# Gated mix of dilated window attention and full attention: row-maxima products of the projection stage on 32 rows of the array instead of 64

## The chip, the cores and the metric

One Trainium2 chip, one core of it. The metric is the device time of one execution in microseconds (us). Engines are named as in the profile: PE is TensorE's matmuls and PEld its weight loads, DVE is VectorE, ACT is ScalarE, POOL is GpSimd, SP is SyncE, which issues the DMAs.

## The reference: what is computed

`x` is 2048 tokens by 448 features. Two attention blocks with 16 heads of 28 read the same `x`, each with its own `wqkv` and `wo`. Block A lets a token see 8 earlier tokens, two apart; block B is full attention. A gate per token mixes them.

```python
def _A_ref(x, wqkv, wo):            # W, dil = 8, 2
    ...
    idx = pos[:, None] - off[None, :]        # off = arange(8) * 2
    logits = jnp.einsum("bhsd,bhswd->bhsw", q, kg) * scale
    ...
def _B_ref(x, wqkv, wo):
    ...
    scores = jnp.einsum("bhqd,bhkd->bhqk", q, k) * (Dh ** -0.5)
    p = _softmax(scores, axis=-1)
    o = jnp.einsum("bhqk,bhkd->bhqd", p, v)
    ...
x = A_x
g = _sigmoid((x * gate_w).sum(-1, keepdims=True))
return g * _A_ref(x, A_wqkv, A_wo) + (1 - g) * _B_ref(x, B_wqkv, B_wo)
```

## The kernel before, in words

The kernel writes the order of every engine by hand. It has two long stages on PE, and a short end in which the two output projections run beside the last attention steps.

**Projection stage.** `x` and the weights are split into a high and a low part (`xh`, `xl`, `wh`, `wl`), and a product of the two is the sum of three products, so a tile of 128 output rows takes 11 matmuls (the list `ORDER`; four of 128 input features for high by high, four for low weights, three for low inputs). There are 92 tiles: 28 for queries and keys of block B (`"qk"`, 512 columns, line 293), 16 for its values (`"v"`, 448 columns, line 298) and 48 for block A (`"a"`, 448 columns, line 298). The first 10 tiles (`FULL`) run as matmuls over all 128 rows of the array. From tile 10 on `project_halves` cuts every product into two of 64 input features: one uses the array's rows 0 to 63 and writes `PJ[n % 2][:, 0, :]`, the other uses rows 64 to 127 and writes `PJ[n % 2][:, 1, :]`. Two lists (`todo[0]` and `todo[1]`, one for each half of the array) are popped in turn, so consecutive matmuls use different halves. For two tiles there are 21 products in each list. ACT then copies both sums out of PSUM, and POOL adds them.

**Row maxima.** Block B's softmax subtracts, per query, the maximum of its scores over the keys. These maxima come from products of their own (`s1`), one matmul for 128 queries by 512 keys of one head, 1024 in all, on the high parts alone. Number `n` is divided into a block `u` of 512 queries and four heads, 128 queries of it, 512 keys of it, and a head `h = n % 4`. Each result is 512 wide in PSUM, and DVE reduces it to one number per query in `MX`. 320 of the 1024 run in the projection stage, four for each of the 80 tiles 12 to 91; the other 704 run in the attention stage.

In the attention stage a maxima product reads the 28 rows of its head: `slice(32 * h, 32 * h + DH)`. In the projection stage it reads 64 rows: heads 0 and 1 lie in rows 0 to 63 of `KH`, heads 2 and 3 in rows 64 to 127, and the queries lie in two tiles, `QP[..][0]` with heads 0 and 2 and `QP[..][1]` with heads 1 and 3, whose other rows are zero. So a product over 64 rows sums one head alone. `s1_half(k, half)` issues one such matmul for head `k + 2 * half` into `PM[k][:, half, :]`. It stands in list `half`: `k = 0` after two products of the tile, `k = 1` after eight entries. When both halves have issued their `k`, DVE reduces `PM[k]`, two heads by 512, in one instruction (line 162).

**Attention stage.** 256 steps, each with 12 score matmuls over 28 or 30 rows (line 1022; four heads, three products each), up to three maxima products over 28 rows (line 144), then eight matmuls of probabilities by values over 128 rows and 32 columns (line 976, two for each of four heads). ACT exponentiates the scores (line 1025), DVE reduces maxima (line 148), and POOL does block A. The end projects with `wo` (line 815, 128 rows).

Of the kernel before, what the change touches and what calls it, by code (L numbers as in the profile page):

```python
# [11 lines left out]
ALU = mybir.AluOpType  # L12
X = mybir.AxisListType.X
ET = mybir.EngineType

S, D, H, DH = 2048, 448, 16, 28
# [5 lines left out]
NMX = 192  # L22
# [3 lines left out]
def gated_mix_kernel(ctx: ExitStack, tc: tile.TileContext, xT, xn, gw, wA, wB, woAB, out):  # L26
    nc = tc.nc
# [26 lines left out]
    PJ, PM = PS[0:2], PS[2:4]  # L54
# [20 lines left out]
    MX = cp.tile([128, NMX], F32, name="MX")  # L75
# [13 lines left out]
    half = {}  # L89
# [37 lines left out]
    s1c = [0]  # L127
    s1e = 64 * NU
    finished = []

    def load_qhi(u):
        g, b = divmod(u, NB)
        qhis[u] = QP[u % 2]
        for h in range(4):
            r = 112 * g + DH * h
            dma_r(qhis[u][h % 2][32 * h:32 * h + DH, :], qk_hi[r:r + DH, 512 * b:512 * b + 512])

    def s1_mm(n, bank, half=False):
        u, i = divmod(n, 64)
        qs, kc, h = i // 16, i // 4 % 4, i % 4  # L140
        if i == 0 and u + 1 < NU:
            load_qhi(u + 1)
        r = slice(64 * (h // 2), 64 * (h // 2) + 64) if half else slice(32 * h, 32 * h + DH)
        nc.tensor.matmul(bank, qhis[u][h % 2][r, 128 * qs:128 * qs + 128],  # L144
                         KH[u // NB % 3][r, 512 * kc:512 * kc + 512], start=True, stop=True)

    def s1_max(n, k, bank):
        r = nc.vector.tensor_reduce(MX[:, n % NMX:n % NMX + k], bank, axis=X, op=ALU.max)  # L148
        if n // 64 != (n + k) // 64:
            finished.append(n // 64)  # L150
        s1c[0] = n + k
        return r.ins


    def s1_half(k, half):
        n = s1c[0]
        s1_mm(n + k + 2 * half, PM[k][:, half, :], True)
        halves[k] += 1
        if halves[k] == 2:
            halves[k] = 0  # L160
            m = MX[:, n % NMX:n % NMX + 4].rearrange("p (a b) -> p a b", b=2)[:, :, k]
            nc.vector.tensor_reduce(m, PM[k], axis=X, op=ALU.max)  # L162
            if k == 1:
                s1c[0] = n + 4
                if s1c[0] % 64 == 0:
                    finished.append(n // 64)

    halves = [0, 0]

# [12 lines left out]
    def max_turn(t):  # L184
        r = sp.tile([128, 32], F32, name="nms")
        nc.vector.transpose(r, t)
        return r
# [18 lines left out]
    with tc.tile_pool(name="xp", bufs=1) as xp, tc.tile_pool(name="wp", bufs=2) as wp:  # L206
# [103 lines left out]
        def project_halves(n, s1):  # L310
            if n % 2 == 0:
                for m in (n, n + 1):
                    low = (tiles[m][2] if tiles[m][1] == "qk" else tiles[m][-1] // 4) < 2
                    for half in range(2):
                        l = [p for p in ORDER if p != (0, 1, 3) or half == (0 if low else 1)]
                        l = [(m, product, (m, p, half, i == 0, i == len(l) - 1)) for i, p in enumerate(l)]
                        if s1[m - n]:
                            late = m == S1_START
                            l[8 + late:8 + late] = [(m, s1_half, (1, half))]
                            l[2 + 4 * late:2 + 4 * late] = [(m, s1_half, (0, half))]  # L320
                        todo[half] += l
            while any(l and l[0][0] == n for l in todo):
                for l in todo:
                    if l:
                        _, f, x = l.pop(0)
                        f(*x)
# [83 lines left out]
        r, t = xst[:, 0, 0:3, :], xst[:, 0, 3, :]  # L410
# [7 lines left out]
        for kt in range(3):  # L418
            nc.vector.tensor_tensor(out=xl[0][:, kt, :], in0=r[:, kt, :], in1=xh[0][:, kt, :].bitcast(F32),
                                    op=ALU.subtract)  # L420
        nc.vector.tensor_tensor(out=tail[64:128], in0=t[64:128], in1=tail[64:128].bitcast(F32), op=ALU.subtract)
        nc.vector.tensor_tensor(out=wl0[:, 3, 0:256], in0=wt0[:, 0:256], in1=wh0[:, 3, 0:256].bitcast(F32),
                                op=ALU.subtract)
# [27 lines left out]
        for n, t in enumerate(tiles):  # L451
# [4 lines left out]
            for w in splits:  # L456
                i, k = (n - splits[w][0]) * splits[w][1], splits[w][1]
# [6 lines left out]
            if n < FULL:  # L464
                project(n)
            else:
                project_halves(n, [S1_START <= m < S1_START + 80 for m in (n, n + 1)])
# [41 lines left out]
            if n == 70:  # L509
                r = max_turn(omw)  # L510
# [175 lines left out]
    for c in range(8):  # L686
# [20 lines left out]
        n = 0  # L707
# [10 lines left out]
    late = {"pool": 0.0, "dve": 0.0}  # L718
# [186 lines left out]
    for u in range(NU - 1):  # L905
        f = NJ * (u + 1)
        l = {NU - 3: (1, 2, 5, 6, 9, 12, 13, 15), NU - 2: (1, 2, 5, 6, 8, 10, 10, 12)}.get(
            u, (1, 3, 6, 8, 12, 18, 19, 22) if u < NU - 5 else (1, 3, 6, 8, 12, 15, 16, 19))
# [88 lines left out]
    def scores(u, kt, cur):  # L997
# [10 lines left out]
        for tok in WITH if k else ALONE:  # L1008
            if tok[0] == "s":
                i = int(tok[1])  # L1010
                if i < k:
                    s1_mm(n + i, bank[tok])
                if i == 0:
                    s1_max(n, 1, T1)
                elif i == 2 and k > 1:
                    r = s1_max(n + 1, k - 1, other[:, 0:k - 1, :])
                    apart(r, other)
                continue
            a, t = tok[0], int(tok[1])
            h = (int(a) + n) % 4  # L1020
            r = slice(32 * h, 32 * h + (DH + 2 if t == 0 else DH))
            nc.tensor.matmul(bank[a], (KH[g % 3], KH[g % 3], KL[g % 2])[t][r, ks], (qh, ql, qh)[t][r, :], start=(t == 0), stop=(t == 2))  # L1022
            if t == 2 and a in "20":
                p = probs[len(exps) % 8]
                e = nc.scalar.activation(p, RP[0] if a == "2" else mine, AF.Exp, scale=SCALE).ins  # L1025
                if len(exps) >= 8:
                    tc.declare_no_dep(e, exps[-8], reason="the matmuls that read it came between")
                exps.append(e)
                if a == "0":
                    apart(e, mine)  # L1030
                cur[(h + 3) % 4], cur[h] = p[:, 0, :], p[:, 1, :]
                yield len(cur)
# [17 lines left out]
    for u in range(NU):  # L1050
        g, b = divmod(u, NB)
# [62 lines left out]
    for j in range(12, 16):  # L1114
# [4 lines left out]
        bank = acc[j - 12]  # L1119
# [40 lines left out]
```

## Time and profile before

| | us |
|---|---|
| median of 3 runs (lowest, highest) | 914.49 (913.26, 914.99) |
| the profiled execution | 912.73 |
| its span, first to last instruction | 911.0 |
| PE busy | 903.8 (99%) |
| DVE busy | 731.7 (80%) |
| ACT busy | 652.2 (72%) |
| POOL busy | 620.6 (68%) |

The profiled execution is 1.76 us below the median, and 1.73 us of it lie outside its span. A PE record runs from the start of a matmul to the modelled end of its results, so records overlap and a busy PE is not a PE at its peak; the distance from start to start is what a matmul costs. A PEld record is the load of weights that stands ahead of every matmul. Shapes such as 64\*128 are rows by columns of the array that the instruction uses. In a timeline, consecutive instructions of the same kind are merged into one row with their count, and a bracket names the idle time before the row and what ended it; "issue" means that nothing that the profile shows was waited for.

### The profile page before, as it was taken

The page shows a single profiled execution, that of the slowest core. Times are in us where ns is not written, and L with a number is a line of the kernel's source. Part 1 is how long each engine was busy: PE and PEld are TensorE (multiplying, and loading weights), DVE is VectorE, ACT ScalarE, POOL GpSimd, SP SyncE. Part 2 cuts the span into 40 slices and gives each one's busy share as a digit, 9 for nine tenths or more (in the row PEclk, how much of TensorE's full clock was granted, in tenths as well). Part 3 has the DMA queues.
Part 4 walks back from the last instruction along what each step waited for, and adds up shares of the span by engine and source line. Part 5 has one row for each costly group of instructions (what it writes and reads, how often), then busy time and mean ns, then how long its engine had stood idle before and what let it go on. Part 6 is the DMA issues. An engine that isn't in the chain of part 4 may idle for free.

```text
span 911.0 us, 20699 instructions
## 1 busy us (share of the span) xinstructions
PE 903.8 (99%) x8396; PEld 536.3 (59%) x8396; DVE 731.7 (80%) x977; ACT 652.2 (72%) x802; POOL 620.6 (68%) x485
## 2 busy tenths in 40 slices
PE   9999999999999999999999999999999999999998
PEld 7889999999944444444444444444444444466667
DVE  6488999999989998999999999999998888401012
ACT  6456434343388898888888888888989989855551
POOL 2489846564469799998999999999996762300100
PEclk9999999999999999999999999999999999999999
DMA  9977403554373331426135242341311223554422
GB/s 266 294 260 197 133 12 89 155 132 117 82 244 91 95 103 45 113 82 143 34 109 146 82 103 73 96 111 44 92 44 36 55 69 100 143 162 120 134 83 91
DMA packets 101119, 104.29 MB, mean 114 GB/s; under 512 B 61652, under 2 KB 71252, under 8 KB 100240
## 3 DMA queue, kind: packets, MB, share of 16 engines
q1 hardware_dynamic: 100880, 102.72, 39.8%
q8 instruction: 65, 1.06, 0.5%
q10 hardware_dynamic: 144, 0.26, 0.1%
q14 instruction: 30, 0.25, 0.1%
HBM read 61.99 MB, written 40.48 MB: 112 GB/s over the span
## 4 chain that ended last, share of the span: by engine, by line
PE 95%; DMA 1%; ACT 1%; SPq 1%; DVE 0%; issue 0%; POOL 0%; ACTq 0%; DVEq 0%; POOLq 0%
PE T L1022 29%; PE av L976 27%; PE r L298 15%; PE T L815 8%; PE r L293 7%; PE r L144 4%; PE T L144 4%; ACT P L1025 1%; PE T L793 1%; DMA V<-in_xT 1%; DMA onlo<-on_lo 1%; SPq L101 0%; DMA rs<-finv 0%; SPq L854 0%; ACT wo L758 0%
## 5 line engine op out<-in xcount | busy, mean ns | idle before, releaser
L1025 ACT ACTIVATE P<-T 128x1024 f32<-128x1024 f32 x512 | 497.7, 1026 | 81.9 <-PE T L1022 80.3
L148 DVE TENSOR_REDUCE MX<-T 128x1 f32<-128x512 f32 x470 | 441.5, 954 | 31.2 <-PE T L144 18.7
L976 PE MATMUL av<-P,V 128*32 128x512 f32 x2048 | 272.7, 605 | 0.3
L1022 PEld LDWEIGHTS T<-QH,KH 30*128 30x128 f32 x1024 | 90.8, 181 | 221.2 <-ACT P L1025 198.2
L144 PE MATMUL T<-KH,QP 28*128 28x512 f32 x704 | 219.6, 454 | 0.3 <-DVE MX L162 0.3
L1022 PE MATMUL T<-QH,KH 30*128 30x512 f32 x1024 | 212.0, 489 | 1.2 <-ACT P L1025 1.1
L162 DVE TENSOR_REDUCE MX<-r 128x2 f32<-128x1024 f32 x160 | 192.6, 1221 | 24.6 <-PE r L144 22.9
L1022 PE MATMUL T<-QH,KL 28*128 28x512 f32 x1024 | 186.4, 396 | 0.0
L1022 PE MATMUL T<-QL,KH 28*128 28x512 f32 x1024 | 184.1, 392 | 0.0
L611 POOL TENSOR_TENSOR prod<-qt,kt 128x896 f32<-128x896 f32 x64 | 135.1, 2114 | 1.8 <-DMA kt<-a_scr 1.8
L362 ACT ACTIVATE raw<-r 128x896 f32<-128x896 f32 (+1 forms) x64 | 58.9, 921 | 97.8 <-PE r L298 96.5
L666 POOL TENSOR_TENSOR oat<-oat,prod 128x896 f32<-128x896 f32 x56 | 118.2, 2110 | 2.3
L144 PEld LDWEIGHTS T<-KH,QP 28*128 28x128 f32 x704 | 86.0, 181 | 27.3 <-ACT P L1025 22.0
L661 POOL TENSOR_TENSOR prod<-vt,L 128x896 f32<-128x896 f32 x56 | 95.4, 1704 | 0.4
L363 POOL TENSOR_TENSOR ast<-raw 128x448 f32<-128x448 f32 x48 | 55.4, 1154 | 58.2 <-ACT raw L362 47.1
L1022 PEld LDWEIGHTS T<-QL,KH 28*128 28x128 f32 x1024 | 93.4, 184 | 0.0
L1022 PEld LDWEIGHTS T<-QH,KL 28*128 28x128 f32 x1024 | 91.9, 183 | 0.9
L976 PEld LDWEIGHTS av<-P,V 128*32 128x32 f32 x2048 | 40.3, 108 | 77.6 <-issue 72.5
L298 PE MATMUL r<-wh,xh 64*128 64x448 f32 (+1 forms) x512 | 83.5, 362 | 0.0
L144 PE MATMUL r<-KH,QP 64*128 64x512 f32 x320 | 83.1, 390 | 0.0
L803 DVE TENSOR_TENSOR oalo<-T,oah 128x384 fp32r<-128x384 f32 x16 | 8.9, 557 | 90.8 <-ACT onhi L802 87.7
L298 PE MATMUL r<-wh,xl 64*128 64x448 f32 (+1 forms) x384 | 69.4, 363 | 0.0
(110 smaller groups left out, 1104.0 us busy)
## 6 DMA issues: line engine op xcount, KB each, us to landing
a_scr<-ast SPq DMA_DIRECT2D x24, 448.0 KB
qk_hi<-qkh SPq DMA_DIRECT2D x24, 256.0 KB
qk_lo<-qkh SPq DMA_DIRECT2D x24, 256.0 KB
rbc<-rs SPq DMA_DIRECT2D x60, 64.0 KB
QP<-qk_hi SPq DMA_DIRECT2D x64, 56.0 KB
KL<-qk_lo SPq DMA_DIRECT2D x16, 224.0 KB
QH<-qk_hi SPq DMA_DIRECT2D x64, 56.0 KB
QL<-qk_lo SPq DMA_DIRECT2D x64, 56.0 KB
```

Source lines behind the costliest of these rows:

```text
L144: nc.tensor.matmul(bank, qhis[u][h % 2][r, 128 * qs:128 * qs + 128], KH[u // NB % 3][r, 512 * kc:512 * kc + 512], start=True, stop=True)
L148: r = nc.vector.tensor_reduce(MX[:, n % NMX:n % NMX + k], bank, axis=X, op=ALU.max)
L162: nc.vector.tensor_reduce(m, PM[k], axis=X, op=ALU.max)
L293: nc.tensor.matmul(bank, ws[c][rows, k, t[4]:t[4] + 128], x, start=first, stop=last)
L298: nc.tensor.matmul(bank[:, 0:cols], x, ws[c][rows, k, 0:cols], start=first, stop=last)
L611: nc.gpsimd.tensor_tensor(out=p, in0=qt[c], in1=kvt["k", c % 2][:, HALO - DIL * w:HALO - DIL * w + NJ, :], op=ALU.mult)
L661: nc.gpsimd.tensor_tensor(out=dst.rearrange("p j (h d) -> p j h d", d=DH), in0=kvt["v", c % 2][:, HALO - DIL * w:HALO - DIL * w + NJ, :].r ...
L666: nc.gpsimd.tensor_tensor(out=oat[c], in0=oat[c], in1=oat[c, w], op=ALU.add)
L815: writes(bank, nc.tensor.matmul(bank[:, :D], src, wo[c][:, k, :], start=(first and k == ks[0] and i == 0), stop=(last and k == ks[-1] and ...
L976: nc.tensor.matmul(av[32 * h:32 * h + 32, :], V[:, kt, 4 * g + h, :], tiles_[h], start=(kt == 0), stop=(kt == NJ - 1), skip_group_check=True)
L1022: nc.tensor.matmul(bank[a], (KH[g % 3], KH[g % 3], KL[g % 2])[t][r, ks], (qh, ql, qh)[t][r, :], start=(t == 0), stop=(t == 2))
L1025: e = nc.scalar.activation(p, RP[0] if a == "2" else mine, AF.Exp, scale=SCALE).ins
```

## The change

It touches the 320 maxima products of the projection stage. `s1_mm` loses its argument `half` and always reads the 28 rows of its head, so that these matmuls use 32 rows of the array, a quarter, in place of 64. `s1_half` is replaced by `s1_two(half)`: it issues two of them one behind the other, heads `2 * half` and `2 * half + 1`, into the two banks of `PM[half]`, and the reduction of that pair follows at once. List 0 of a tile carries `s1_two(0)` after two products, and list 1 carries `s1_two(1)` after eight. (In tile 12 the places are six and nine, as before.) Each list of a tile had two maxima entries of one matmul; now it has one entry of two matmuls. The number of matmuls, their 512 columns, and the number and sizes of DVE's reductions stay; the reduction writes two neighbouring columns of `MX` in place of every other column. `QP` keeps its two tiles with the zero rows; the rows that are zero are no longer read here.

```diff
-    def s1_mm(n, bank, half=False):
+    def s1_mm(n, bank):
...
-        r = slice(64 * (h // 2), 64 * (h // 2) + 64) if half else slice(32 * h, 32 * h + DH)
+        r = slice(32 * h, 32 * h + DH)
...
-    def s1_half(k, half):
+    def s1_two(half):
         n = s1c[0]
-        s1_mm(n + k + 2 * half, PM[k][:, half, :], True)
-        halves[k] += 1
-        if halves[k] == 2:
-            halves[k] = 0
-            m = MX[:, n % NMX:n % NMX + 4].rearrange("p (a b) -> p a b", b=2)[:, :, k]
-            nc.vector.tensor_reduce(m, PM[k], axis=X, op=ALU.max)
-            if k == 1:
-                s1c[0] = n + 4
-                if s1c[0] % 64 == 0:
-                    finished.append(n // 64)
-
-    halves = [0, 0]
+        for i in range(2):
+            s1_mm(n + i, PM[half][:, i, :])
+        s1_max(n, 2, PM[half])
...
-                            l[8 + late:8 + late] = [(m, s1_half, (1, half))]
-                            l[2 + 4 * late:2 + 4 * late] = [(m, s1_half, (0, half))]
+                            i = 8 + late if half else 2 + 4 * late
+                            l[i:i] = [(m, s1_two, (half,))]
```

PE's order in the tiles of 448 columns, before, over two tiles. `KH` and `QP` mark maxima products, `wh`, `wl`, `xh`, `xl` products of the projection; `r_128` and `r_132` are the projection's sums, `r_136` and `r_140` are `PM[0]` and `PM[1]`, and matmuls that follow each other alternate between the halves of the array.

```order
L144 MATMUL r_136<-KH_152,QP_155 128x512 x2
L298 MATMUL r_128<-wh_2337,xh_181 128x448 x4
L298 MATMUL r_128<-wl_2338,xh_181 128x448 x7
L298 MATMUL r_128<-wh_2337,xl_185 128x448
L144 MATMUL r_140<-KH_152,QP_156 128x512 x2
L298 MATMUL r_128<-wh_2337,xl_185 128x448 x5
L298 MATMUL r_132<-wh_2337,xh_183 128x448 x4
L144 MATMUL r_136<-KH_152,QP_155 128x512 x2
```

The same place of PE's order in the changed kernel.

```order
L144 MATMUL r_136<-KH_152,QP_155 128x512
L144 MATMUL r_136<-KH_152,QP_156 128x512
L289 MATMUL r_128<-wh_2337,xh_181 128x448 x4
L289 MATMUL r_128<-wl_2338,xh_181 128x448 x6
L289 MATMUL r_128<-wh_2337,xl_185 128x448
L289 MATMUL r_128<-wl_2338,xh_181 128x448
L144 MATMUL r_140<-KH_152,QP_155 128x512
L144 MATMUL r_140<-KH_152,QP_156 128x512
L289 MATMUL r_128<-wh_2337,xl_185 128x448 x5
L289 MATMUL r_132<-wh_2337,xh_183 128x448 x5
L144 MATMUL r_136<-KH_152,QP_155 128x512
L144 MATMUL r_136<-KH_152,QP_156 128x512
```

Both orders visit the maxima four times in two tiles, with two matmuls at each visit. Before, the two are one head of each half of the array (one tile of `QP`); now they are both heads of the same half (both tiles of `QP`). Between the visits stood 12 or 9 products, now 12 or 10.

PE's order in the query and key tiles, before, from the end of one tile into the next; the names are as above.

```order
L293 MATMUL r_132<-xh_183,wl_414 128x512 x7
L293 MATMUL r_132<-xl_187,wh_413 128x512
L144 MATMUL r_140<-KH_151,QP_156 128x512 x2
L293 MATMUL r_132<-xl_187,wh_413 128x512 x5
L293 MATMUL r_128<-xh_180,wh_413 128x512 x4
L144 MATMUL r_136<-KH_151,QP_155 128x512 x2
```

And in the changed kernel.

```order
L284 MATMUL r_132<-xh_183,wl_414 128x512 x6
L144 MATMUL r_140<-KH_151,QP_155 128x512
L144 MATMUL r_140<-KH_151,QP_156 128x512
L284 MATMUL r_132<-xl_187,wh_413 128x512 x6
L284 MATMUL r_128<-xh_180,wh_413 128x512 x4
L144 MATMUL r_136<-KH_151,QP_155 128x512
L144 MATMUL r_136<-KH_151,QP_156 128x512
```

Here too a visit is two matmuls of one half, with ten products to the next. DVE's order has the same 911 rows before and after, with the reductions of `r_136` and `r_140` in turn.

## The prediction

> **What bounds the kernel now.** First the windows view: busy time of every engine in the maxima part of the projection stage (query and key tiles, then the tiles of 448 columns), the attention stage and the end.
>
> ```profile
> core 0: us, PE busy (x) PEld busy (x) DVE busy (x) ACT busy (x) POOL busy (x), PEclk, DMA share, GB/s
> 39.50:85.50 46.00, 46.00 (x399) 41.52 (x397) 38.35 (x32) 26.37 (x40) 42.76 (x38) 1.00 0.78 239
> 85.50:252.30 166.80, 166.80 (x1596) 161.52 (x1593) 154.36 (x140) 67.44 (x89) 97.21 (x104) 1.00 0.38 105
> 252.30:790.00 537.70, 535.97 (x5443) 222.60 (x5440) 501.89 (x727) 478.85 (x544) 466.21 (x326) 1.00 0.35 94
> ```
>
> PE is busy in every microsecond of the first two windows at full clock (1.00); DVE comes next with 154.36 of 166.80. Busy alone does not prove the bound, so I read the chain that ended last, in order of time, once for each kind of tile.
>
> ```profile
> 48.01 1.40 PE r L293 x12
> 49.41 0.24 PE r L144 x2
> 49.65 0.94 PE r L293 x8
> ...
> 53.82 1.40 PE r L293 x12
> ...
> 130.25 1.23 PE r L298 x12
> 131.47 0.23 PE r L144 x2
> 131.70 0.82 PE r L298 x8
> ...
> 135.47 1.23 PE r L298 x12
> ```
>
> The chain stays on PE with no wait in it. Two tiles take 53.82 - 48.01 = 5.81 us at 512 columns and 135.47 - 130.25 = 5.22 us at 448. Twelve half products take 1.40 or 1.23 us, so two of them, one on each half of the array, share a slot of 0.23 or 0.205 us; two maxima products share one of 0.23 us. Whatever PE gains or loses here moves everything behind it.
>
> **What is removed.** A tile loses four maxima products over 64 rows, two slots; the stage loses four slots in two tiles, one for each visit to the maxima in PE's new order. That is 160 slots of 0.23 us, 36.8 us.
>
> **What is added.** 160 visits of two matmuls over 28 rows, with 64-row products ahead and behind. If such a pair could run in its half while the other half projects, it would take half a slot. The trace has one place where 28- or 30-row matmuls follow 64-row ones, at the end of the stage. The rows around it, then from narrower windows the last three 64-row matmuls and the last by itself:
>
> ```profile
> 251.64 0.41 PE L144 MATMUL r<-KH,QP 64*128 64x512 f32 x2
> 251.88 0.78 PE L298 MATMUL r<-wh,xl 64*128 64x448 f32 x5
> 251.88 0.39 PEld L298 LDWEIGHTS r<-wh,xl 64*128 64x128 f32 x3
> 252.58 0.18 PEld L1022 LDWEIGHTS T<-QH,KH 30*128 30x128 f32 x2 [0.32 <-issue]
> 252.59 0.50 PE L1022 MATMUL T<-QH,KH 30*128 30x512 f32 x2
> ...
> 252.08 0.58 PE L298 MATMUL r<-wh,xl 64*128 64x448 f32 x3
> ...
> 252.29 0.36 PE L298 MATMUL r<-wh,xl 64*128 64x448 f32 x1
> ```
>
> Inside the stage a weight load starts while the preceding matmul runs (251.88 for both engines). Here the loads wait until 252.58, 0.29 us after the last 64-row matmul started, where the next product would have followed after 0.205; and nothing that the profile shows held them ("issue"). That last matmul used one half only. The other half's last one is among the three from 252.08 on, a slot earlier, and the two loads behind go to one row group in each half (heads 1 and 2 of `scores` at n = 320). The load for the free half waited too. So I read it as PE emptying itself when the height of the row groups changes. Two other changes look the same: 128 to 64 rows at tile 10, and 28 rows to the 128 by 32 shape of line 976; the row of a last matmul stands ahead of the load that follows.
>
> ```profile
> 33.05 0.40 PE L293 MATMUL r<-xl,wh 128*128 128x512 f32 x1
> 33.37 0.53 PEld L293 LDWEIGHTS r<-xh,wh 64*128 64x128 f32 x6 [0.36 <-issue]
> ...
> 788.78 0.40 PE L1022 MATMUL T<-QH,KL 28*128 28x512 f32 x2
> 789.10 0.16 PEld L976 LDWEIGHTS av<-P,V 128*32 128x32 f32 x8 [0.37 <-issue]
> ```
>
> Both loads come 0.32 us after the start of a 512-wide matmul. The second part of the price is the load itself, which no longer hides. From the groups by shape, in a window over the stage with its last change at the end:
>
> ```profile
> L144 PE MATMUL r<-KH,QP 64*128 64x512 f32 x320 | 83.1, 390 | 0.0
> L1022 PE MATMUL T<-QH,KH 30*128 30x512 f32 x2 | 0.5, 495 | 0.0
> ```
>
> Of the same width, the first matmuls behind a change have records of 495 ns, those in the stream 390: 0.105 us in which the weights still come in.
>
> The trace never shows a return from 28 to 64 rows, half of what is added. Its price is bounded below by the slot itself, as if the products simply went on, and above by the largest change shown, 0.32 us plus the load; I take the latter, because the change from 28 rows to another shape (788.78 to 789.10) is the nearest row. The Trainium skill says in TensorEngine Tiling (Array Packing), section Tiling Modes, that changing the tiling mode, and not just the tile, drains TensorE; by that sentence the return costs the same as the way in.
>
> Step by step, for a visit between 448-wide products: 0.29 us from the last product's start to the maxima's loads; 0.105 for the loads; 0.32 from the start of the two maxima matmuls to the products' loads; 0.105 for those. Sum 0.82 us from one product slot to the next, which before was 0.205: 0.615 added. Between 512-wide products it is 0.32 + 0.105 + 0.32 + 0.105 - 0.23 = 0.62, the same. The removed slot of 0.23 goes off: 0.385 us net for a visit, and 160 of them give **61.6 us**. That the two matmuls of a visit overlap follows from the attention stage, where the pair of line 1022 at 252.59 shares one record's length. Between the visits stand 12 or 10 products, even numbers, so no half of the array is left with a slot of its own.
>
> **What hides it: nothing.** Who queues behind a visit on PE are the products of both halves, then ACT's copies and POOL's additions; they wait longer and have room, since PE releases them already. DVE does the same reductions:
>
> ```profile
> L162 DVE TENSOR_REDUCE MX<-r 128x2 f32<-128x1024 f32 x160 | 192.6, 1221 | 24.6 <-PE r L144 22.9
> ```
>
> Four of 1.221 us in two tiles are 4.88 of 5.22 us now and would be of about 6.76, so `PM` comes free earlier, measured in PE's work, than before. No DMA is moved past another; loads issued by tile number come later together with their tiles. The attention stage starts later by the whole sum and is otherwise the same. Its clock stays 1.00 in spite of two such changes in every step, so I add nothing for the clock.
>
> The sum against the profiled execution is 912.73 + 61.6 = 974.3 us. That execution was 1.76 us below the median, so against the median it is 976.1. Bounds for this case: with 0.29 us for every change and the mean load of 489 - 396 = 93 ns from the two rows below, a visit is 0.766 - 0.435 = 0.33 net, 53 us in all, 967; with 0.035 us more for a change, for halves that stop apart, it is 0.455, 73 us, 987.
>
> ```profile
> L1022 PE MATMUL T<-QH,KH 30*128 30x512 f32 x1024 | 212.0, 489 | 1.2 <-ACT P L1025 1.1
> L1022 PE MATMUL T<-QH,KL 28*128 28x512 f32 x1024 | 186.4, 396 | 0.0
> ```
>
> **Rivals.**
>
> *Different halves never wait for each other (faster).* Mechanism: only row groups that overlap conflict, and the wait at 252.58 has a cause that the profile lacks. Then a visit takes one half for a slot while the other projects, and two tiles lose 2 x 0.23 = 0.46 us of PE. Query and key tiles take all of it, 8 pairs of tiles x 0.46 = 3.7. In the other 32 pairs DVE's 4.88 us become the limit, and 5.22 - 4.88 = 0.34 x 32 = 10.9 is what comes. Time 914.5 - 14.6 = 899.9. It decides as soon as a 28-row load starts before the other half's product has ended. For it: the halves do run independently while both use 64 rows. Against it: the load for the free half at 252.58. The Trainium skill, in TensorE: Matmul & The Clock Gate, Part 3, What overlaps and what doesn't, has weight loads overlap matmuls in flight whenever their row groups differ; by that rule alone this rival would hold, and the trace speaks against it at that one place.
>
> *Weights load during the emptying.* Each of 320 changes is cheaper by 0.105: 33.6 less, 942.5. Against it are the records of 495 ns.
>
> *Only the way into 28 rows empties PE.* A visit then costs 0.29 + 0.105 - 0.205 = 0.19 for entering and half a slot, 0.115, for itself, less the removed 0.23: 0.075 x 160 = 12 us, 926.5; if the way in costs a little less, nothing is left of it and the time is unchanged.
>
> *The change does not run two heads at once.* If the second matmul of a visit waits for the first, another 0.23 x 160 = 36.8 us come on top: 1012.9. Against it are the two that start together at 252.59.
>
> **How the numbers follow.** The forecast has 0.80: three changes of shape in three places show the same two prices, and one is of the very kind. The faster rival has 0.09, loads during the emptying 0.04, one way only 0.05, heads one by one 0.02. Within 0.2% counts as no change, about what a measurement of this kernel can tell. Faster 0.09; same 0.02, the cheap end of the one-way rival; slower 0.89. The forecast alone spans 967 to 987; the range goes down to 940 to take in the loads that overlap, and ends at 990. It leaves out 0.16.
>
> **What would show it.** In the changed profile's timeline of the stage, each maxima load should start 0.29 us after the last product before it, with both halves silent, and records of about 495 ns should stand at the first matmuls of 28 rows and of 64 rows alike. Two tiles should take 5.22 + 4 x 0.385 = 6.76 us, or 7.35 at 512 columns; DVE's share in the stage should fall; the attention stage should keep its 538 us. I am wrong if a product of one half starts between a visit's loads and its results: then the halves are independent. If the waits are there but the records behind them stay at 390 ns, the load was hidden and the price is a half of mine.

## The result, and the profile after

| | before | after |
|---|---|---|
| median, us | 914.6 | 975.92 |
| lowest, highest (4 runs each) | 913.26, 914.99 | 975.56, 978.49 |
| ratio, 95% interval | | 1.0681, 1.0666 to 1.0697 |
| profiled execution | 912.73 | 978.49 |
| its span | 911.0 | 976.7 |

The change is slower by 61 us. The forecast was 61.6 us more: 976.1 us against the median of before, 974.3 us against its profiled execution.

First, where the time went. The windows view of the changed kernel, cut at about the same places of the program as before: the query and key tiles with a little of what follows, the rest of the projection stage, the attention stage.

```profile
core 0: us, PE busy (x) PEld busy (x) DVE busy (x) ACT busy (x) POOL busy (x), PEclk, DMA share, GB/s
39.50:102.00 62.50, 62.50 (x426) 37.23 (x422) 41.64 (x35) 29.02 (x45) 48.92 (x43) 1.00 0.68 202
102.00:316.10 214.10, 214.10 (x1572) 138.23 (x1570) 155.72 (x137) 64.67 (x84) 91.02 (x99) 1.00 0.27 75
316.10:854.00 537.90, 536.36 (x5444) 223.18 (x5443) 501.72 (x727) 479.46 (x544) 466.25 (x326) 1.00 0.35 94
```

The attention stage keeps its 538 us. PE still reads as busy throughout the projection stage, because its records reach over the gaps between matmuls; what betrays the gaps is PEld, 138 of 214 us, where before it had 162 of 167, and DVE, which falls from 93% to 73%. The ends of the stage are the first 64-row matmul and the first score matmul, each a row of the timeline; the first row here is the kernel before, the others are the changed kernel.

```profile
33.38 0.50 PE L293 MATMUL r<-xh,wh 64*128 64x512 f32 x2
...
33.82 0.50 PE L284 MATMUL r<-xh,wh 64*128 64x512 f32 x2
...
316.17 0.50 PE L1013 MATMUL T<-QH,KH 30*128 30x512 f32 x2
```

That is 316.17 - 33.82 = 282.35 us, where before it was 252.59 - 33.38 = 219.21: 63.1 us more. The rest of the 65.7 us between the two spans is 0.4 ahead of the stage and about 2 at the very end of this one execution, behind the last computation:

```profile
961.07 9.74 PE T L806 x48
970.82 0.04 DVEq L813
970.85 0.04 issue
970.90 0.62 DVE res L813
```

Its last result is computed at 971.52 and its span ends at 976.7, 5.2 us later; before it was 3.1. The other three runs took 975.56 to 976.21, about 2 us less.

Second, the mechanism. Two visits in the timeline of the changed kernel, first PE's matmuls, then the weight loads with the idle time ahead of them.

```profile
123.49 0.78 PE L289 MATMUL r<-wl,xh 64*128 64x448 f32 x6
124.19 0.50 PE L144 MATMUL r<-KH,QP 28*128 28x512 f32 x2
124.62 0.88 PE L289 MATMUL r<-wh,xl 64*128 64x448 f32 x6
125.34 0.57 PE L289 MATMUL r<-wh,xh 64*128 64x448 f32 x4
125.84 0.50 PE L144 MATMUL r<-KH,QP 28*128 28x512 f32 x2
126.27 0.47 PE L289 MATMUL r<-wh,xh 64*128 64x448 f32 x2
```

```profile
124.19 0.18 PEld L144 LDWEIGHTS r<-KH,QP 28*128 28x128 f32 x2 [0.31 <-issue]
124.62 0.51 PEld L289 LDWEIGHTS r<-wh,xl 64*128 64x128 f32 x6 [0.24 <-issue]
125.14 0.39 PEld L289 LDWEIGHTS r<-wh,xh 64*128 64x128 f32 x4
125.84 0.18 PEld L144 LDWEIGHTS r<-KH,QP 28*128 28x128 f32 x2 [0.31 <-issue]
126.26 0.19 PEld L289 LDWEIGHTS r<-wh,xh 64*128 64x128 f32 x2 [0.24 <-issue]
```

Both visits have idle time in the loads on both sides, and "issue" says that the profile shows nothing else that was waited for. Over the whole stage the profile puts a part of the idle time ahead of the maxima loads down to DVE:

```profile
L144 PEld LDWEIGHTS r<-KH,QP 28*128 28x128 f32 x318 | 29.3, 181 | 51.0 <-issue 29.9 <-DVE MX L148 20.8 <-DMA qk_hi<-qkh 0.4
```

DVE does not set it. From the start of the last product to the load it takes the same time under both names: behind 448-wide products 0.294 us at the median of the 96 visits named "issue" and 0.295 at that of the 32 named DVE, and behind 512-wide products 0.32 us under either name. In the fifth experiment below, whose reductions are short, no load is put down to DVE, and the distances are the same 0.295 and 0.32 us. At the two visits shown, the visit's two matmuls start together, and no product of either half starts until 0.43 us later. From one visit to the next, over ten products, it takes 1.65 us. The group of the maxima matmuls shows that the weights' load is paid at each of them, 495 ns in place of 390; the DVE group shows whom it does not hurt.

```profile
L144 PE MATMUL r<-KH,QP 28*128 28x512 f32 x320 | 79.9, 495 | 0.0
...
L148 DVE TENSOR_REDUCE MX<-r 128x2 f32<-128x1024 f32 x160 | 196.0, 1225 | 83.4 <-PE r L144 82.9
```

The reductions take the same 1.22 us, and DVE now waits 83 us for PE where it waited 23. PE's chain over two tiles, with 512 and then with 448 columns:

```profile
49.52 1.36 PE r L284 x10
...
56.90 1.36 PE r L284 x9
...
126.33 1.46 PE r L289 x11
127.79 0.43 PE r L144
128.22 1.22 PE r L289 x10
129.44 0.43 PE r L144 x2
...
133.16 1.46 PE r L289 x11
```

Two tiles take 56.90 - 49.52 = 7.38 us where 7.35 were forecast, and 133.16 - 126.33 = 6.83 where 6.76 were. A visit is a piece of 0.43 us, not a slot of 0.23.

### The profile page after: what moved, and what is told of

The parts are those of the page before. It is cut to its first block, busy times and chain, and to the rows that moved or that the text cites. A ratio compares the mean times of both kernels' runs of the same rounds, so it can differ in the third digit from the quotient of the medians.

```text
span 976.7 us, 20707 instructions
## 1 busy us (share of the span) xinstructions
PE 967.4 (99%) x8396; PEld 508.5 (52%) x8396; DVE 736.1 (75%) x977; ACT 651.7 (67%) x802; POOL 620.6 (64%) x485
## 4 chain that ended last, share of the span: by engine, by line
PE 94%; DMA 2%; ACT 1%; SPq 1%; DVE 0%; issue 0%; POOL 0%; ACTq 0%; DVEq 0%; POOLq 0%
PE T L1013 27%; PE av L967 25%; PE r L289 17%; PE T L806 7%; PE r L144 7%; PE r L284 7%; PE T L144 4%; DMA V<-in_xT 1%; ACT P L1016 1%; PE T L784 1%; DMA onlo<-on_lo 1%; SPq L101 0%; DMA rs<-finv 0%; DVE xl L206 0%; DMA rs<-osb 0%
## 5 line engine op out<-in xcount | busy, mean ns | idle before, releaser
L148 DVE TENSOR_REDUCE MX<-r 128x2 f32<-128x1024 f32 x160 | 196.0, 1225 | 83.4 <-PE r L144 82.9
L289 PE MATMUL r<-wh,xh 64*128 64x448 f32 (+1 forms) x512 | 86.1, 389 | 0.0
L144 PE MATMUL r<-KH,QP 28*128 28x512 f32 x320 | 79.9, 495 | 0.0
```

The source lines that it names most:

```text
L289: nc.tensor.matmul(bank[:, 0:cols], x, ws[c][rows, k, 0:cols], start=first, stop=last)
```

## The experiments

Each kernel was timed against runs of the kernel before on the same chip; their median was 912.97 us for the first four experiments and 913.83 for the last three.

**Rows alone.** The order of before with 28 rows, so that a visit has one matmul in each half:

```diff
-        r = slice(64 * (h // 2), 64 * (h // 2) + 64) if half else slice(32 * h, 32 * h + DH)
+        r = slice(32 * h, 32 * h + DH)
```

> The order of the kernel before (each visit to the maxima is one head of each half of the array) with only the rows changed, 28 instead of 64. Theory (PE empties itself when the height of the row groups changes, 0.82 us from product to product at each visit): as slow as the changed kernel, and a little slower, because 12 and 9 products stand between the visits, and 9 leaves one half idle for a slot: 80 such slots of 0.1 us are about 8 us more, so 984 us, 976 to 992. Rival (what costs is that both matmuls of a visit sit in one half, so that the other half has nothing to do): about the time before, 914 to 920.

Measured: 984.64 us, ratio 1.078 (1.0764 to 1.0796). Its loads, in the same view as above:

```profile
124.92 0.18 PEld L144 LDWEIGHTS r<-KH,QP 28*128 28x128 f32 x2 [0.31 <-issue]
125.35 0.30 PEld L298 LDWEIGHTS r<-wh,xh 64*128 64x128 f32 x4 [0.25 <-issue]
```

The same two gaps, now with one head in each half. So the cost does not come from both matmuls of a visit lying in one half. Nor does it come from where their rows begin: the visits take heads 0 and 2, which begin where the halves begin, and heads 1 and 3, which begin 32 rows further, in turn, and from the last product's start to the load it is 0.29 us at both kinds (0.32 behind 512 columns). The odd number of products costs about what was expected: the stage takes 323.60 - 33.84 = 289.76 us, 7.4 more than in the changed kernel, where 8 had been worked out.

**Grouping alone.** The changed kernel with 64 rows again, and each head an entry of its own:

```diff
-    def s1_mm(n, bank):
+    def s1_mm(n, bank, half=False):
...
-        r = slice(32 * h, 32 * h + DH)
+        r = slice(64 * (h // 2), 64 * (h // 2) + 64) if half else slice(32 * h, 32 * h + DH)
...
-    def s1_two(half):
+    def s1_one(half, i):
         n = s1c[0]
-        for i in range(2):
-            s1_mm(n + i, PM[half][:, i, :])
-        s1_max(n, 2, PM[half])
+        s1_mm(n + i, PM[half][:, i, :], True)
+        if i:
+            s1_max(n, 2, PM[half])
...
-                            l[i:i] = [(m, s1_two, (half,))]
+                            l[i:i] = [(m, s1_one, (half, 0)), (m, s1_one, (half, 1))]
```

> The grouping of the changed kernel (two heads of one half, reduced together) with 64 rows with zeros as before, each head an entry of its own in the list of its half. No height changes. Theory: the time before, 914.6 us within 1%. Rival (the grouping costs): most of the 61 us, 950 or more.

Measured: 913.83 us, ratio 1.0001 (0.9989 to 1.0012). Pairing two heads of one half, and the reduction with it, costs nothing.

**Twice the visits.** The kernel of the first experiment, with the entries of the second list moved by two or three places, so that no two maxima matmuls meet:

```diff
-                            l[8 + late:8 + late] = [(m, s1_half, (1, half))]
-                            l[2 + 4 * late:2 + 4 * late] = [(m, s1_half, (0, half))]
+                            i = 8 + late + 2 * half
+                            l[i:i] = [(m, s1_half, (1, half))]
+                            i = 2 + 4 * late + 3 * half
+                            l[i:i] = [(m, s1_half, (0, half))]
```

> 28 rows, and every maxima matmul alone at its place, with 2 to 8 products ahead and behind: 320 visits of one matmul in place of 160 of two; the number of matmuls is the same. Theory: the price is paid for a visit; by the changed kernel's two tiles a visit adds 0.62 us, 320 x 0.62 - 36.8 = 162 us, so 1076 us, 1065 to 1085. Rival (the price belongs to each matmul over 28 rows): as the changed kernel, 976.

Measured: 1075.41 us, ratio 1.1775 (1.1758 to 1.1793). The same 320 matmuls cost 162 us over the time before in 320 visits and 61 in 160. A visit of one:

```profile
126.44 0.49 PE L144 MATMUL r<-KH,QP 28*128 28x512 f32 x1
126.86 0.67 PE L298 MATMUL r<-wh,xh 64*128 64x448 f32 x4
```

It takes 0.42 us, as much as a visit of two. The price belongs to the change of height and not to the single matmul.

**Half the visits.** The changed kernel with the four heads of a tile in one place, in list 0 of even tiles and list 1 of odd ones:

```diff
-    def s1_two(half):
+    def s1_four():
         n = s1c[0]
-        for i in range(2):
-            s1_mm(n + i, PM[half][:, i, :])
-        s1_max(n, 2, PM[half])
+        for i in range(4):
+            s1_mm(n + i, PM[i // 2][:, i % 2, :])
+        for i in range(2):
+            s1_max(n + 2 * i, 2, PM[i])
...
-                            i = 8 + late if half else 2 + 4 * late
-                            l[i:i] = [(m, s1_two, (half,))]
+                            if half == m % 2:
+                                l[6:6] = [(m, s1_four, ())]
```

> 28 rows, and the four heads of a tile at one place, on all four quarters: 80 visits of four matmuls. Theory: PE alone 80 x 0.62 - 36.8 = 13 us over the time before, 927; but both reductions, 2.45 us, now start together and the next visit needs their banks, so that a tile can't be shorter than about 3.05 us, which gives 945. Between 925 and 950. Rival (a price for each matmul): 976. Rival (an idle half costs): 900 to 915, since no half is idle in a visit.

Measured: 934.86 us, ratio 1.0236 (1.0219 to 1.0253), between the two figures that were worked out. The matmuls of two visits and DVE's reductions around them:

```profile
121.04 0.77 PE L144 MATMUL r<-KH,QP 28*128 28x512 f32 x4
...
124.21 0.50 PE L144 MATMUL r<-KH,QP 28*128 28x512 f32 x4
...
118.91 2.35 DVE L148 TENSOR_REDUCE MX<-r 128x2 f32<-128x1024 f32 x2 [0.78 <-PE r L144]
121.58 2.35 DVE L148 TENSOR_REDUCE MX<-r 128x2 f32<-128x1024 f32 x2 [0.32 <-PE r L144]
```

At 124.21 all four matmuls fit into one record's length. At 121.04 two of them are 0.27 us late: they write the bank whose reduction ends at 118.91 + 2.35 = 121.26. The visits are not evenly spaced, and only the shorter gap is too short for DVE. I had taken DVE's time for the length of every tile; it binds in every second one.

**Half the visits, short reductions.** As above, with seven eighths of each maximum left out, so that DVE is out of the way:

```diff
-            s1_max(n + 2 * i, 2, PM[i])
+            s1_max(n + 2 * i, 2, PM[i][:, :, 0:64])
```

> The run with four heads at one visit, with DVE's reductions cut to the first 64 of 512 keys, which leaves out seven eighths of the maximum. Theory: with four heads at a visit every second visit waited for a bank that DVE still read, 0.27 us each; without that wait only PE's price is left, 80 x 0.62 - 36.8 = 13 us over the time before, 926 us (922 to 929). Rival (four matmuls in flight cost more by themselves, and DVE's wait hid behind that): no change from 935.

Measured: 927.35 us, ratio 1.0144 (1.0129 to 1.0159). Its chain over two tiles:

```profile
119.80 0.44 PE r L144 x4
120.24 2.44 PE r L290 x21
122.68 0.44 PE r L144 x3
123.12 2.24 PE r L290 x20
125.36 0.44 PE r L144 x4
```

Two tiles take 5.56 us against 5.22 before, and a visit of four is a piece of 0.44 us, a visit of two 0.43, a visit of one 0.42. So 80, 160 and 320 visits cost 13.5 (with the short reductions), 61 and 162 us. Even at one visit for a tile, all four quarters at work, the visit with its two changes costs more than the two slots that it saves.

**60 rows.** The kernel before with four rows of zeros fewer:

```diff
-        r = slice(64 * (h // 2), 64 * (h // 2) + 64) if half else slice(32 * h, 32 * h + DH)
+        r = slice(64 * (h // 2), 64 * (h // 2) + 60) if half else slice(32 * h, 32 * h + DH)
```

> The kernel before, with the maxima products of the projection stage over 60 rows instead of 64 (the four rows left out hold zeros on the query side). Theory: what counts is the class of height that the rows need (32, 64 or 128), and 60 rows need the same as 64, so nothing is emptied: the time before within 0.3%, 912 to 917 us. Rival (any difference in the number of rows empties PE): as the run with the order of before and 28 rows, 984.

Measured: 914.92 us, ratio 1.001 (0.9999 to 1.002).

```profile
L144 PE MATMUL r<-KH,QP 60*128 60x512 f32 x318 | 79.9, 394 | 0.6 <-DMA KH<-qk_hi 0.6
```

The records have 394 ns where 64 rows had 390 and 28 rows 495, so the loads are hidden: 60 rows stream among 64 rows without a gap. A different number of rows alone does no harm; 60 go with 64, as 28 go with 30 in the attention stage (28-row records of 396 ns, in the prediction).

**Fewer visits in the attention stage.** The attention stage changes shape twice in each step. Here the matmuls of probabilities by values run for two steps at once:

```diff
-            if prev is not None:
-                do_av(prev)
-            prev = (kt, cur, g)
+            if len(prev) == 2:
+                do_av(prev.pop(0))
+                do_av(prev.pop(0))
+            prev.append((kt, cur, g))
```

> The kernel before, with the projection stage untouched; in the attention stage the matmuls of probabilities by values run for two steps at once, in every second step, so that 256 visits to the 128 by 32 shape become 128. Theory, if nothing else binds there: a visit saved is about 0.4 us, 128 x 0.4 = 51 us less, 863 us; the least that ACT and DVE allow is about 35 us less, since DVE is busy 502 of the stage's 538 us, so 880 to 890. Rival (the visits hide ACT's exponentials, which PE's scores wait for): with two visits in a row PE waits for ACT in the next step instead, and the time is the same or up to 60 us longer.

Measured: 1005.39 us, ratio 1.1 (1.0984 to 1.1016), worse than the rival's worst; neither forecast held. ACT's exponentials in this kernel, then in the kernel before:

```profile
400.95 4.02 ACT L1025 ACTIVATE P<-T 128x1024 f32<-128x1024 f32 x4 [1.27 <-PE T L1022]
406.24 4.03 ACT L1025 ACTIVATE P<-T 128x1024 f32<-128x1024 f32 x4 [1.27 <-PE T L1022]
```

```profile
401.00 1.95 ACT L1025 ACTIVATE P<-T 128x1024 f32<-128x1024 f32 x2
402.82 0.64 ACT L887 ACTIVATE onhi<-on 128x512 fp32r<-128x512 f32 x1
403.34 1.95 ACT L1025 ACTIVATE P<-T 128x1024 f32<-128x1024 f32 x2
405.58 1.94 ACT L1025 ACTIVATE P<-T 128x1024 f32<-128x1024 f32 x2 [0.29 <-PE T L1022]
```

Two steps take 406.24 - 400.95 = 5.29 us in place of 405.58 - 401.00 = 4.58; 0.71 for each of 128 pairs would be 91 us, as much as the whole loss. ACT idles 1.27 us while PE does both visits, and then PE waits for ACT in the step that has none:

```profile
406.24 1.03 ACT P L1025
407.27 0.04 issue
407.32 0.49 PE T L1022
```

Here the changes stand in time that ACT needs anyway, so fewer of them gained nothing; what a change costs in this stage the run does not show. No version here beats the kernel before.

## Why the prediction was right

- **The bound.** PE's chain without a wait was the right place to cost the change: the stage grew by 63.1 us, the whole by 61, and the attention stage stayed.
- **PE empties itself when the height changes.** This hung on one place in the trace, the load for the free half at 252.58. The changed kernel shows it at its visits, and the first experiment shows that it holds with one matmul in each half too. The signs that the prediction named compare the start of one record with the end of another, and can't be read off: ends are modelled, and by them the loads at 124.19 start 0.08 us before the last products end (123.49 + 0.78 = 124.27). Starts decide: the maxima's loads come 0.29 us behind the last products' start, where the next product would have come after 0.205, and the half that the visit leaves free starts nothing from 124.19 to 124.62, 0.43 us, although its next product stands right behind the two maxima in PE's order. The rival in which the halves are independent is out. By the Trainium skill's page TensorEngine Tiling (Array Packing), section Tiling Modes, a change of mode drains TensorE; the idle times of 0.31 and 0.24 us agree. The rule of the Trainium skill's page TensorE: Matmul & The Clock Gate, Part 3, The mechanism, that a load is pulled ahead of matmuls in flight when its row group does not conflict with theirs, did not hold here between groups of different height: the load for the free half waited until 124.62. The section of the Trainium skill that the prediction names, What overlaps and what doesn't, has it only the other way round: loads overlap matmuls in flight only when the row groups differ. That the two other changes in the prediction "show the same two prices" says too much: its rows for them show the wait alone, and the price of the load only at line 1022.
- **The way back costs the same.** It had been taken from the nearest row. From the visit's matmuls to the products' loads the trace has 124.62 - 124.19 = 0.43 us, which is the 0.105 and 0.32 of the sum. The rival in which only the way in costs is out. It had been the less certain half of the sum, taken at its upper bound.
- **The loads are not hidden**: 495 ns for 320 matmuls, and on the way back 0.47 us for the two 448-wide products at 126.27, where such a product has 0.36 in the stream (252.29 in the prediction). That rival, and the one in which two heads run one after the other, are out as well; the row at 124.19 has both in 0.50 us.
- **Sizes.** A visit came out at (6.83 - 5.22) / 4 = 0.40 us net at 448 columns and at 63.1 / 160 = 0.39 over the whole stage, where 0.385 were forecast: 1.5 us in 160 visits. The bounds of 0.33 and 0.455 held it, though the prediction gives no row for the 0.035 us in the upper one, and no run shows that term. That the medians agree with the sum within 0.2 us is partly luck: the stage alone was off by 1.5, and the four runs of the changed kernel lie 2.9 us apart.
- **DVE** got room, as argued, and waits 60 us longer for PE. Where I did forecast DVE as a bound, in the fourth experiment, I was off by half: a mean over tiles hid that the visits were unevenly spaced.

## What to carry to other kernels

In these runs matmuls over row groups of different height did not share the array: a visit of 28 rows among 64-row products held up both halves, while 60 rows among 64 held up none. Count the changes of height, not the matmuls. A change cost about 0.2 us: 0.09 behind the slot of the last matmul (0.29 - 0.205, or 0.32 - 0.23), and 0.105 of a weight load that no longer hides. Twice the visits confirm it: each visit more added (162 - 61) / 160 = 0.63 us, which is a slot of 0.23 for its own matmul and 0.40 for two changes. If small contractions must stand among larger ones, pad them with zeros to the larger height, which is what the kernel before does. Gathering them would pay only where a visit saves more than its two changes cost, and no run here reached that. And before removing such changes elsewhere, look at what other engine uses the time: in the attention stage it was ACT.

## What the runs showed of the hardware that was not expected

A visit costs nearly the same with one, two or four matmuls of 28 rows in it: 0.42, 0.43 and 0.44 us from its start to the next product's load. So a change of height, once paid, leaves the other quarters of the array free. What PE does in the 0.31 and 0.24 us in which no weights load was not tried; that it streams out its last results is a reading of the starts, not something that the profile shows.
